# A fused linear-attention and mixture-of-experts kernel: W2's splits behind the first batch's gates, and two first-layer steps ahead of the projection's second part

## The chip, the cores and the metric

The kernel runs on one core of a Trainium2 chip. The metric is the device time of one execution in microseconds. Three runs of the kernel before took 406.46, 407.17 and 407.32 us, a median of 407.17 us. The execution that was profiled took 406.74 us.

## The reference

Eight batches of 576 tokens and 8 heads pass through an attention with 32 memory slots, and each token then goes to the one best of 8 experts.

```python
a = softmax(phi, axis=2)                       # over the 576 tokens
k_m, v_m = einsum(a, k), einsum(a, v)          # 32 slots per head
attn = softmax(q @ k_m.T / 8)                  # over the 32 slots
x = (attn @ v_m), heads side by side           # [4608, 512]
logits = xn @ en.T / tau                       # x and the 8 expert vectors, normed
expert_idx = argmax(logits); gate_w = softmax(logits)[expert_idx]
out[mask] = gate_w[mask] * (relu(x[mask] @ w1[e]) @ w2[e])
```

Inputs and outputs are fp32: w1 is 8 x 512 x 1024, w2 is 8 x 1024 x 512.

## The kernel before, in words

**One batch, one expert.** The kernel treats each batch as if all its tokens went to one expert (`choose` takes the fullest one; `rest` repairs the others at the end). Since x is a product of attention weights and v_m, the first layer is computed as weights times (v_m times W1): `project` makes the product G of v_m and W1 in two parts of 512 columns each (PSUM tiles pg), and `first` multiplies it with the turned attention weights aT.

**Three matmuls for one fp32 product.** G, aT, the hidden layer and W2 are each split in a high part, rounded to a shorter format, and a low part, the difference: gh and gl, the two aT tiles, hh and hl, wh and wl. A product is high times high, high times low and low times high. `split_w` makes one of the eight row blocks of wh by a copy and of wl by a subtraction, both from w2s; `part` does the same for aT.

**Steps.** `first(b)` has 16 steps: two halves of 288 tokens by eight blocks of 128 hidden units. Step f of the first half needs the columns of G from 128 f on, so steps 0 to 3 need only the first part of the projection. Each ends in an ACT copy with Relu (hh), in the second half another (h4, the last 64 tokens), and a DVE subtraction (hl). `second(b)` has 40 steps: eight for the last 64 tokens, which use w2s and h4 unsplit, then eight for each of four tiles of 128 tokens, which use wh, wl, hh and hl. `must(f)` makes a block of W2's split if the list has not yet done so.

**What stands between the steps.** `steps` fills two lists, `first` and `second`, with calls that are made behind the step of that number. They hold the rest of this batch's routing (`attend`, `norm`, `late`: norms, root, gates) and the next batch's attention: scores (ts, tl), their softmax over the slots in x on DVE and ACT (`fill` L64, `weigh` L71, L73, L75, `divide` L83 to L86), the turn into aw (`turn` L92, L94), and a copy of x by way of DRAM into ea (`lay`: eight td writes L100, then ea reads L104 and L106, which wait for all eight writes). Two batches ahead it takes the softmax of phi in ex (`largest` L457, `softmax` L472). `visit` turns ex on PE (L504) and multiplies aw with the values (`pairs` L139); `gather` chooses the next batch's expert (`choose`: ki L208, seli L209) and then calls for its weights: SP reads seli and issues four loads of W1 (w1s, L442) and four of W2 (w2s, L448).

**What sets the order.** The order in which the program calls is the order on each engine: PE, DVE, ACT, POOL (GpSimd) and SP, which issues nearly all DMAs, each take their own instructions strictly in that order and wait for semaphores. So on SP the ea reads, the two stores of `keep` (ad L633, vd L634) and the read of seli stand ahead of the next batch's W1.

**Before the change, batch 0.** Both parts of the projection and the attention of tiles 1 and 2 come ahead of the first step. Blocks 0 and 1 of W2 are split on POOL behind step 2, ahead of the gates' idx (L263); blocks 2 to 7 stand behind steps 9 to 14 on POOL, with the copies of 6 and 7 on ACT. The softmax of phi for batch 2 stands behind steps 18 and 21 of `second`.

Of the kernel before, what the change touches and what calls it, by code (L numbers as in the profile page):

```python
# [8 lines left out]
F32 = mybir.dt.float32  # L9
# [4 lines left out]
ALU = mybir.AluOpType  # L14
# [5 lines left out]
P = 128  # L20
B, H, S, D, M = 8, 8, 576, 64, 32
N, DM, E, FF = B * S, H * D, 8, 1024
NG = 2
# [5 lines left out]
HS = S // 2  # L29
# [246 lines left out]
class Kernel:  # L276
# [368 lines left out]
        for g in range(NG):  # L645
            self.part(g, slice(0, S))

    def split_w(self, copy=None):
        j = self.halves
        x, h, l = self.w2s[:, j], self.wh[:, j], self.wl[:, j]  # L650
        (copy or self.nc.scalar.copy)(h, x)  # L651
        self.nc.gpsimd.tensor_tensor(out=l, in0=x, in1=h.bitcast(F32), op=ALU.subtract)  # L652
        self.halves += 1

    def project(self, n, vT, room=None):
# [87 lines left out]
    def steps(self, b, t, u):  # L743


        first, second = ([[] for _ in range(n)] for n in (16, 40))

        for j in range(8):
            at = first[j] if b else first[2] if j < 2 else first[7 + j]
            at.append(lambda j=j: self.split_w(self.nc.gpsimd.tensor_copy if b or j < 6 else None))  # L750
        if not b:
            late = t.late()
            first[2].append(lambda: t.attend(3, 4))
            first[3].append(lambda: t.norm(3, 4))
            first[4] += [t.total, lambda: self.load_kv(2)]

            for f in range(3, 9):
                first[f].append(lambda: next(late))
            first[12] += [lambda: self.keep(0), lambda: self.load_q(2)]
        if u:  # L760
            c, o = b + 1, 0 if b else 3
            if not b:
                first[9].append(lambda: self.scores(c))
            for k in range(2):
                first[(3 + k if b else 9 + 2 * k)].append(lambda k=k: self.results(c, k))

            places = (first[6], first[8], first[10], first[12]), (first[12], first[14], second[0], second[3])
            if not b:
                places = (second[3], second[3], second[3], second[7]), (second[7], second[7], second[7], second[10])
            all = slice(0, BL)  # L770
            for g in range(NG):
                work = u.weigh((g,), all)
                places[g][0].append(lambda g=g: u.fill((g,), all, [self.sT[:, i] for i in range(NG)]))
                for at in places[g][1:]:
                    at.append(lambda work=work: next(work, None))
            for at, g in zip((second[0], second[3]) if b else (second[7], second[10]), range(NG)):
                at.append(lambda g=g: (u.divide((g,), all), u.lay(g), u.turn((g,), all)))
            o = 0 if b else 7
            m = b + 2
            if m < B:  # L780
                for g in range(NG):
                    second[11 + 3 * g + o].append(lambda g=g: self.softmax(m, (g,)))
                second[16 + o].append(lambda: self.shares(m))
                second[17 + o].append(lambda: self.visit(u, m))
                second[(20 if b else 19) + o].append(lambda: self.gather(u, m))
                second[(28 if b else 25) + o].append(lambda: self.load_phi(m + 1))
                second[(31 if b else 28) + o].append(lambda: self.load_kv(m + 1))
            else:
                second[17].append(u.attend)
                second[20].append(lambda: self.load_w2(u.choose()))  # L790
                second[37].append(lambda: list(self.project(c, self.vT[c % 2], self.pt)))
            o = 0 if b else 2
            second[22 + o] += [self.parts, lambda: self.keep(c)]
            second[23 + o + (not b)] += [u.owner, u.flags]
            for n, i in enumerate(((0, 1), (2, 3), (4,))):
                second[24 + n + o + (not b)].append(lambda i=i: u.norm(*i))
            after = u.late()
            for n in (27, 28, 29, 30, 31, 32):
                second[n + o].append(lambda: next(after))
            second[32 + o].append(lambda: list(after))  # L800
        return first, second
# [19 lines left out]
    def batch(self, b, t, u):  # L821

        first, second = self.steps(b, t, u)
        self.halves = 0

        def must(f):
            while self.halves <= f:
                self.split_w()

        if b and u:  # L830
            self.keys(b + 1)
            self.values(b + 1)
        for k, _ in enumerate(self.project(b, self.vT[b % 2]) if u else ()):
            if not b:
                for g in range(NG):
                    self.part(g, slice(HS, S) if k else slice(P, HS), self.nc.scalar.copy)
                if k:
                    t.norm(1, 2)
                else:
                    self.keys(1)  # L840
                    self.values(1)
                    t.attend(1, 2)
        if b and u:

            self.scores(b + 1)
        for n, _ in enumerate(self.first(b)):
            for step in first[n]:
                step()
        for n, _ in enumerate(self.second(b, self.gate[:, b], self.rows(b), must)):
            for step in second[n]:  # L850
                step()
            if n == 8 and b == B - 1:
                left = self.others()
            if n == 24 and b == B - 1:
                self.tc.mark_branch_hint_location("others", left[1], engines=[ET.PE, ET.DVE, ET.SP, ET.Activation])
        return left if b == B - 1 else None
# [244 lines left out]
```

## Time and profile before

| what | value |
|---|---|
| median of three runs | 407.17 us (406.46 to 407.32) |
| the profiled execution | 406.74 us, its span 404.9 us |
| granted clock of TensorE, mean | 0.998 of 2.4 GHz |
| PE busy | 393.5 us, 97% of the span |
| DVE busy | 262.3 us, 65% |
| ACT busy | 157.2 us, 39% |
| POOL busy | 171.2 us, 42% |
| moved by DMA | 91.24 MB, 225 GB/s on average |

The times in all rows are microseconds from the span's start. A batch takes about 45 us of it, and batch 0's first layer begins at 32.4 us. A matmul's end in the profile is modelled, so the start of the next one tells more than the end of the one before.

### The profile page before, as it was taken

To read this page: it belongs to the slowest core of one execution; us is meant where nothing else is said; L and a number is where in the kernel's file an instruction comes from. 1 tells how busy PE (TensorE), PEld (TensorE's weight loads), DVE (VectorE), ACT (ScalarE), POOL (GpSimd) and SP (SyncE) were. 2 spreads that over 40 slices of the span, in tenths; PEclk is the share of its full clock that TensorE was granted. 3 is DMA by queue.
4 is the path that set the end of the run, shared out by engine and by line. 5 is a ranking of instruction groups with operands and counts; after the bars stand their busy time and mean duration, and the time that the engine had idled before them with its cause. 6 is when DMAs were issued, how large, how long until landed. Compare 5 with 4: busy or idle time off the path is not lost. (4 is left out here: it accounts for less than half of the span.)

```text
span 404.9 us, 10350 instructions
## 1 busy us (share of the span) xinstructions
PE 393.5 (97%) x3933; PEld 318.5 (79%) x3933; DVE 262.3 (65%) x909; ACT 157.2 (39%) x430; POOL 171.2 (42%) x205
## 2 busy tenths in 40 slices
PE   7889999999999999999999999999999999999995
PEld 3458877798777978879787888879788897879784
DVE  4698795769664794758855795747936595745000
ACT  4366623165313633147311753137231561146110
POOL 1036563187133940369121961349303681329300
PEclk9999999999999999999999999999999999999999
DMA  8999927995679925995469926798359404790011
GB/s 265 345 363 357 375 61 183 342 358 212 149 255 386 349 46 132 346 384 234 74 215 389 387 82 160 251 388 338 56 137 361 178 2 81 249 396 6 14 53 56
DMA packets 69862, 91.24 MB, mean 225 GB/s; under 512 B 41800, under 2 KB 47688, under 8 KB 69808
## 3 DMA queue, kind: packets, MB, share of 16 engines
q1 hardware_dynamic: 66928, 82.00, 60.9%
q0 software_dynamic: 2688, 8.26, 5.8%
q8 instruction: 32, 0.52, 0.5%
q10 hardware_dynamic: 192, 0.28, 0.2%
q14 instruction: 22, 0.18, 0.1%
HBM read 71.19 MB, written 19.33 MB: 224 GB/s over the span
## 5 line engine op out<-in xcount | busy, mean ns | idle before, releaser
L681 PE MATMUL ph<-aT,gh 128*128 128x288 f32 x512 | 103.2, 297 | 0.0
L734 PE MATMUL py<-wh,hh 128*128 128x512 f32 x248 | 99.3, 400 | 0.0
L734 PE MATMUL py<-wh,hl 128*128 128x512 f32 x248 | 96.7, 390 | 0.0
L734 PE MATMUL py<-wl,hh 128*128 128x512 f32 x248 | 96.7, 390 | 0.0
L652 POOL TENSOR_TENSOR wl<-w2s,wh 128x512 fp32r<-128x512 f32 x64 | 85.1, 1330 | 5.0
L681 PEld LDWEIGHTS ph<-aT,gh 128*128 128x128 f32 x512 | 81.8, 188 | 1.7 <-DVE oh L162 0.8
L681 PE MATMUL ph<-aT,gl 128*128 128x288 f32 x256 | 75.4, 294 | 0.0
L687 DVE SCALAR_TENSOR_TENSOR hl<-ph,hh 128x288 fp32r<-128x288 f32 x128 | 55.8, 450 | 22.1 <-ACT hh L684 16.7
L739 ACT ACTIVATE ys<-py,gate 128x512 f32<-128x512 f32 (+1 forms) x39 | 25.1, 642 | 105.3 <-PE py L734 70.3
L684 ACT ACTIVATE hh<-ph 128x288 fp32r<-128x288 f32 x128 | 52.4, 417 | 31.9 <-PE ph L681 31.6
L868 POOL DMA_DIRECT2D out_dram<-ys x28 | 15.5, 553 | 106.1 <-ACT ys L739 69.4
L734 PEld LDWEIGHTS py<-wh,hh 128*128 128x128 f32 x248 | 46.5, 188 | 14.6 <-issue 4.9
L734 PEld LDWEIGHTS py<-wh,hl 128*128 128x128 f32 x248 | 46.6, 188 | 10.1
L734 PEld LDWEIGHTS py<-wl,hh 128*128 128x128 f32 x248 | 46.6, 188 | 9.0
L681 PEld LDWEIGHTS ph<-aT,gl 128*128 128x128 f32 x256 | 48.0, 188 | 0.0
L642 POOL TENSOR_TENSOR aT<-aw,aT 128x576 fp32r<-128x576 f32 (+3 forms) x20 | 23.7, 1204 | 48.4 <-DVE aT L641 42.8
L651 POOL CAST wh<-w2s 128x512 fp32r<-128x512 f32 x62 | 38.6, 622 | 1.0 <-DMA w2s<-w 0.9
L723 PE MATMUL py<-w2s,h 128*64 128x256 f32 x256 | 29.4, 382 | 0.0
L665 DVE TENSOR_TENSOR gl<-pg,gh 128x512 fp32r<-128x512 f32 x32 | 20.0, 684 | 8.7 <-ACT gh L664 8.7
L723 PEld LDWEIGHTS py<-w2s,h 128*64 128x64 f32 x256 | 17.7, 137 | 9.3 <-DVE hl L687 1.0
L472 ACT ACTIVATE ex<-ex,nm 128x576 f32<-128x576 f32 x16 | 12.3, 771 | 29.5 <-DVE nm L457 29.5
L664 ACT CAST gh<-pg 128x512 fp32r<-128x512 f32 x32 | 16.5, 599 | 10.5 <-PE pg L662 10.5
(180 smaller groups left out, 468.9 us busy)
## 6 DMA issues: line engine op xcount, KB each, us to landing
kx<-kv SPq DMA_DIRECT2D x32, 512.0 KB, 7.5
w2s<-w SPq DMA_DIRECT2D x32, 512.0 KB, 9.8
w1s<-w SPq DMA_DIRECT2D x28, 512.0 KB, 6.4
out_dram<-ys POOLq DMA_DIRECT2D x28, 256.0 KB, 6.1
qt<-qT SPq DMA_DIRECT2D x12, 576.0 KB, 8.8
ad<-aw SPq DMA_DIRECT2D x8, 576.0 KB, 12.5
td<-x SPq DMA_DIRECT2D x56, 72.0 KB, 2.1
ea<-td SPq DMA_DIRECT2D x7, 512.0 KB, 4.4
```

The costliest lines, as they stand in the source:

```text
L642: self.nc.gpsimd.tensor_tensor(out=al, in0=a, in1=ah.bitcast(F32), op=ALU.subtract)
L651: (copy or self.nc.scalar.copy)(h, x)
L652: self.nc.gpsimd.tensor_tensor(out=l, in0=x, in1=h.bitcast(F32), op=ALU.subtract)
L664: nc.scalar.copy(self.gh[:, g, f], ps[g])
L665: nc.vector.tensor_tensor(out=self.gl[:, g, f], in0=ps[g], in1=self.gh[:, g, f].bitcast(F32), op=ALU.subtract)
L681: nc.tensor.matmul(p, lhsT=w[:, g, fs], rhs=x[:, g, to], start=g == 0 and k == 0, stop=g == 1 and k == 2)
L684: nc.scalar.activation(self.hh[:, f, to], p, AF.Relu)
L687: nc.vector.scalar_tensor_tensor(out=self.hl[:, f, to], in0=p, scalar=0.0, in1=self.hh[:, f, to].bitcast(F32), op0=ALU.max, op1=ALU.subtract)
L723: nc.tensor.matmul(p[64 * j : 64 * j + 64], lhsT=self.h4[:, f], rhs=self.w2s[:, f, d * j : d * j + d], start=f == 0, stop=f == 7,)
L734: nc.tensor.matmul(p, lhsT=h[:, f, to], rhs=w[:, f], start=f == 0 and k == 0, stop=f == 7 and k == 2)
L739: nc.scalar.activation(y[:, :d], p, AF.Copy, scale=gate[:, i : i + 1])
L868: eng.dma_start(self.out[r : r + P], y)
```

## The change

In batch 0, W2's eight splits move behind steps 11 to 15 of `first` and steps 0 to 2 of `second`. Blocks 0 to 2 are copied by POOL and 3 to 7 by ACT; blocks 0 to 5 are subtracted by POOL and 6 and 7 by DVE. The projection's second part comes behind step 1 of `first`; the norms of tiles 1 and 2 come behind step 0. The late routing steps move by one step. The largest values of phi for batch 2 move from steps 18 and 21 of `second` to steps 0 and 1, and the exponentials to steps 2 and 5. For later batches the order on the engines stays as it was.

```diff
-    def split_w(self, copy=None):
+    def split_w(self, copy=None, by=None):
...
-        self.nc.gpsimd.tensor_tensor(out=l, in0=x, in1=h.bitcast(F32), op=ALU.subtract)
+        (by or self.nc.gpsimd).tensor_tensor(out=l, in0=x, in1=h.bitcast(F32), op=ALU.subtract)
...
-            at = first[j] if b else first[2] if j < 2 else first[7 + j]
-            at.append(lambda j=j: self.split_w(self.nc.gpsimd.tensor_copy if b or j < 6 else None))
+            at = first[j] if b else (first[11:] + second)[min(j, 7)]
+            copy = self.nc.gpsimd.tensor_copy if b or j < 3 else None
+            at.append(lambda j=j, copy=copy: self.split_w(copy, None if b or j < 6 else self.nc.vector))
...
-            first[2].append(lambda: t.attend(3, 4))
-            first[3].append(lambda: t.norm(3, 4))
-            first[4] += [t.total, lambda: self.load_kv(2)]
-
-            for f in range(3, 9):
+            first[3].append(lambda: t.attend(3, 4))
+            first[4] += [lambda: t.norm(3, 4), lambda: self.load_kv(2)]
+            first[5].append(t.total)
+
+            for f in range(4, 10):
                 first[f].append(lambda: next(late))
...
-                    second[11 + 3 * g + o].append(lambda g=g: self.softmax(m, (g,)))
+                    if not b:
+                        second[g].append(lambda g=g: self.largest(m, g))
+                    second[10 + 3 * g if b else 2 + 3 * g].append(lambda g=g: self.softmax(m, (g,)))
...
-        for k, _ in enumerate(self.project(b, self.vT[b % 2]) if u else ()):
-            if not b:
-                for g in range(NG):
-                    self.part(g, slice(HS, S) if k else slice(P, HS), self.nc.scalar.copy)
-                if k:
-                    t.norm(1, 2)
-                else:
-                    self.keys(1)
-                    self.values(1)
-                    t.attend(1, 2)
-        if b and u:
-
-            self.scores(b + 1)
+        project = self.project(b, self.vT[b % 2]) if u else ()
+        if b:
+            list(project)
+            if u:
+                self.scores(b + 1)
+        else:
+            self.part(0, slice(P, HS), self.nc.scalar.copy)
+            next(project)
+            self.part(1, slice(P, HS), self.nc.scalar.copy)
+            self.keys(1)
+            self.values(1)
+            t.attend(1, 2, turned=False)
+            first[0] += [lambda: t.turned(1, 2), lambda: t.norm(1, 2)]
+            first[1].insert(0, lambda: list(project))
+            for g in range(NG):
+                first[1].append(lambda g=g: self.part(g, slice(HS, S), self.nc.scalar.copy))
```

On DVE, at the end of batch 0's first layer: hl of the last step (ph_17), then the next batch's softmax over the slots (sT to x, the largest mx, the difference). The order before is this.

```order
L687 SCALAR_TENSOR_TENSOR hl<-ph_17_816,hh 128x288
L64 STREAM_TRANSPOSE x<-sT 128x576
L71 TENSOR_REDUCE mx_00_837<-x 128x18
L73 TENSOR_TENSOR x<-x,mx_00_837 128x576
L64 STREAM_TRANSPOSE x<-sT 128x576
```

The same place in the changed kernel, where nm is the largest of phi and wl the low part of W2:

```order
L687 SCALAR_TENSOR_TENSOR hl<-ph_17_808,hh 128x288
L457 TENSOR_REDUCE nm_826<-ex 128x1
L652 TENSOR_TENSOR wl<-w2s,wh 128x512
L457 TENSOR_REDUCE nm_826<-ex 128x1
L652 TENSOR_TENSOR wl<-w2s,wh 128x512
L64 STREAM_TRANSPOSE x<-sT 128x576
L71 TENSOR_REDUCE mx_00_843<-x 128x18
L73 TENSOR_TENSOR x<-x,mx_00_843 128x576
```

Two subtractions and the two largest values, which stood behind the whole softmax, now stand ahead of it.

On POOL, in batch 0's first layer, the difference of the two orders: the last two low parts of aT, then the gates' idx and W2's blocks.

```order
 L642 TENSOR_TENSOR aT_86<-aw,aT_85 128x160 x2
 L642 TENSOR_TENSOR aT_86<-aw,aT_85 128x288 x2
-L651 CAST wh<-w2s 128x512
-L652 TENSOR_TENSOR wl<-w2s,wh 128x512
-L651 CAST wh<-w2s 128x512
-L652 TENSOR_TENSOR wl<-w2s,wh 128x512
 L263 TENSOR_SCALAR idx<-m_209 128x5
 L651 CAST wh<-w2s 128x512
```

Two blocks no longer stand ahead of idx. Behind it stand three copies and six subtractions now, where four copies and six subtractions stood.

On PE, between the attention of tiles 1 and 2 (po) and the first layer (ph), before:

```order
L119 MATMUL po_1_520<-vv,aw 128x136 x2
L119 MATMUL po_2_523<-vv,aw 128x136 x2
L172 MATMUL tt_1_526<-ident,aw 128x128 x4
L662 MATMUL pg_10_536<-w1s,vT_80 32x512 x4
L662 MATMUL pg_11_537<-w1s,vT_80 32x512 x4
L681 MATMUL ph_00_556<-aT_85,gh 128x288
```

And in the changed kernel:

```order
L119 MATMUL po_2_523<-vv,aw 128x136 x2
L681 MATMUL ph_00_530<-aT_85,gh 128x288
L681 MATMUL ph_00_530<-aT_86,gh 128x288
L681 MATMUL ph_00_530<-aT_85,gl 128x288
L681 MATMUL ph_00_530<-aT_85,gh 128x288
L681 MATMUL ph_00_530<-aT_86,gh 128x288
L681 MATMUL ph_00_530<-aT_85,gl 128x288
L172 MATMUL tt_1_539<-ident,aw 128x128 x4
```

The first step of the first layer has moved ahead of the turned tile tt, and the projection's second part (pg_10, pg_11) behind the second step. SP's order is unchanged.

## Rows read from the trace of the kernel before

**Rows 1.** Page: busy time, share and instructions of PE.

```profile
PE 393.5 (97%) x3933; PEld 318.5 (79%) x3933; DVE 262.3 (65%) x909; ACT 157.2 (39%) x430; POOL 171.2 (42%) x205
```

**Rows 2.** Waits of PE from 27 us on: us in total, times, longest.

```profile
PE po L504 <- ACT ex L472: 0.6, 2, 0.5
PE tt L172 <- ACT kT L551: 0.4, 1, 0.4
PE pg L662 <- DMA w1s<-w: 0.3, 1, 0.3
PE acc L522 <- issue: 0.2, 1, 0.2
```

**Rows 3.** PE's timeline: start, us, instruction [idle before <-releaser].

```profile
64.40 0.28 PE L504 MATMUL po<-ident,ex 64*128 64x64 f32 x2 [0.46 <-ACT ex L472]
```

**Rows 4.** PE's weight loads for batch 1's projection.

```profile
80.42 0.23 PEld L662 LDWEIGHTS pg<-w1s,vT 64*32 64x32 f32 x10 [0.20 <-DMA w1s<-w]
```

**Rows 5.** DMA issues between 71.9 and 72.3 us: KB each, us to landing.

```profile
w1s<-w SPq DMA_DIRECT2D x1, 512.0 KB, 8.4
```

**Rows 6.** SP's timeline ahead of batch 1's W1.

```profile
58.13 5.12 SPq L100 DMA_DIRECT2D td<-x  x8
65.10 0.39 SPq L104 DMA_DIRECT2D ea<-td  x1
...
68.20 0.62 SPq L634 DMA_DIRECT2D vd<-vT  x1
70.30 2.70 SPq L442 DMA_DIRECT2D w1s<-w  x4
```

**Rows 7.** DVE's timeline, the number of batch 1's chosen expert.

```profile
68.56 0.14 DVE L209 TENSOR_SCALAR seli<-ki 1x1 int32<-1x1 int32 x1
```

**Rows 8.** DVE and SP, the same number and loads for batch 2.

```profile
111.97 0.14 DVE L209 TENSOR_SCALAR seli<-ki 1x1 int32<-1x1 int32 x1
```

**Rows 9.** SP, the loads of W1 for batch 2.

```profile
112.89 1.98 SPq L442 DMA_DIRECT2D w1s<-w  x4
```

**Rows 10.** DVE's timeline from batch 0's last step through batch 1's softmax.

```profile
49.59 0.46 DVE L687 SCALAR_TENSOR_TENSOR hl<-ph,hh 128x288 fp32r<-128x288 f32 x1 [0.47 <-ACT h L686]
49.97 0.77 DVE L64 STREAM_TRANSPOSE x<-sT 128x576 f32<-128x576 f32 x1
50.77 0.75 DVE L71 TENSOR_REDUCE mx<-x 128x18 f32<-128x576 f32 x1
51.56 1.56 DVE L73 TENSOR_TENSOR x<-x,mx 128x576 f32<-128x576 f32 x1
...
54.63 1.51 DVE L73 TENSOR_TENSOR x<-x,mx 128x576 f32<-128x576 f32 x1
56.06 0.74 DVE L83 TENSOR_REDUCE z<-x 128x18 f32<-128x576 f32 x1
...
60.28 0.76 DVE L86 TENSOR_TENSOR x<-x,z 128x576 f32<-128x576 f32 x1
...
61.98 0.71 DVE L457 TENSOR_REDUCE nm<-ex 128x1 f32<-128x576 f32 x1
```

**Rows 11.** POOL's timeline, W2's blocks in batch 0.

```profile
49.31 1.28 POOL L652 TENSOR_TENSOR wl<-w2s,wh 128x512 fp32r<-128x512 f32 x1
...
51.23 1.27 POOL L652 TENSOR_TENSOR wl<-w2s,wh 128x512 fp32r<-128x512 f32 x1
...
52.47 1.81 POOL L652 TENSOR_TENSOR wl<-w2s,wh 128x512 fp32r<-128x512 f32 x1
...
54.24 1.28 POOL L652 TENSOR_TENSOR wl<-w2s,wh 128x512 fp32r<-128x512 f32 x1
```

**Rows 12.** ACT's timeline, the last two steps of batch 0's first layer.

```profile
48.40 0.72 ACT L651 CAST wh<-w2s 128x512 fp32r<-128x512 f32 x1
48.91 0.53 ACT L684 ACTIVATE hh<-ph 128x288 fp32r<-128x288 f32 x1
```

**Rows 13.** PE's timeline, tile 0 of batch 0's second layer, block 5.

```profile
55.85 0.39 PE L734 MATMUL py<-wl,hh 128*128 128x512 f32 x1
```

## The prediction

> **What bounds the kernel now.** I read the page's busy times first: PE is busy for 393.5 of 404.9 us [rows 1], so time is won or lost only where PE stands still. Then PE's waits from the start of batch 0's projection on [rows 2]. After 27 us there are four groups of them, 1.5 us in all. The change reaches two: 0.4 us ahead of tt, and 0.46 us at 64.40 us, where PE wants to turn ex and ACT's exponential is late [rows 3]. If nothing else happened, the change could give back some 0.8 us, 0.2% of the run.
>
> So I looked for waits that almost exist. One stands in PE's weight loads: at 80.42 us batch 1's projection waited 0.20 us for the DMA of W1 [rows 4]. The fourth of W1's four loads was issued at about 72.0 us and landed 8.4 us later, at 80.4 [rows 5]: PE reached it just as it landed. There is no slack, and whatever delays that load delays everything behind it, since PE has no longer waits later on which the loss could be won back.
>
> What releases the load? SP takes its queue in order [rows 6]: the eight td writes of the next batch's softmax x, the last four of them behind the second half's L86; ea at 65.10, which waits until all td writes have landed; ad and vd, the latter's issue ending at 68.82; the reading of seli; W1 at 70.30. The number seli was ready at 68.70 [rows 7]. In batch 2, where SP stands waiting for it, W1 follows 0.78 us after seli is ready (112.89 less 112.11) [rows 8, 9]. By that way W1 could have gone at 69.5 in batch 1; it went at 70.30. So it is SP's own queue, and through td the DVE's softmax, that sets W1's issue. This chain runs from DVE at 60.28+0.76 = 61.04 us [rows 10] over td, ea, ad, vd and seli to W1's landing at 80.4 and PE.
>
> **The change part by part.**
>
> *The first steps ahead of the projection's second part.* The work of PE is the same, in another order; step 0 fills the 0.4 us in which tt waited for a PSUM copy [rows 2]. It needs gh, gl and aT of the first part, which may come 0 to 0.4 us late; gain between 0 and 0.4 us. I take 0.4: PE is then early by that through batch 0.
>
> *POOL.* Two blocks of W2 go from ahead of idx to behind it. DVE loses two stumbles against them, and gains a step's delay of the gates, so I leave idx where it was. The next three pairs then end as before, at 49.31+1.28 = 50.59 us [rows 11], and three bare subtractions of 1.28 us follow: 51.9, 53.2 and 54.4 undisturbed.
>
> *ACT.* One copy of W2 (0.51 us to the next start [rows 12]) goes from ahead of the last hh, and PE is 0.4 us early, so the last hl may start some 0.6 us sooner than 49.59 and end at 49.4 instead of 49.97. Then come four copies in a row at 0.51 us. The last hh (48.91 before [rows 12], some 0.6 us sooner) and its h4 take 0.4 us of ACT, so the first copy starts at about 48.75; that makes block 6's high part ready at 50.5 and block 7's at 51.0. The two exponentials of ex follow and are off the chain.
>
> *DVE.* Two largest values (0.69 us each, by 0.71 of L457 [rows 10]) and two subtractions, for which no row of DVE exists. The nearest is L86, two SBUF inputs and 576 columns: 0.76 us [rows 10]; for 512 columns 0.6 to 0.7 us, I take 0.6. The bound on the other side is what such an operation takes beside POOL: L73, of L86's shape, took 1.56 and 1.51 us [rows 10]. The first started at 51.56 while POOL subtracted from 51.23 to 52.50 and ended 0.62 us after that; the second started at 54.63, POOL ended at 55.52, and it ended 0.62 us later at 56.14. POOL's subtraction in between took 1.81 instead of 1.28 us [rows 11]. So each waits until the other's instruction is over. L64 and L71 kept their 0.77 and 0.75 us beside POOL.
>
> The Trainium skill ("SBUF — State Buffer", section "SBUF: two separate sides") says the same as a rule: VectorE and GpSimd share one pair of ports as an exclusive lock, which a VectorE instruction with two SBUF inputs needs and which is held for a whole instruction. This trace agrees, by the 0.62 us after POOL's end twice. It speaks against giving DVE two of the subtractions while POOL still makes the others: by the rule the sum is the second one below, and without it the first.
>
> First sum, nothing waits for POOL: hl ends 49.4, largest 50.1, subtraction from 50.5 (block 6's high part) to 51.1, largest 51.8, subtraction 52.4, then 0.80, 0.79 and 0.70 us twice for L64, L71 (start to start [rows 10]) and L73 (L86's 0.76 less a short overlap with the next): 57.0, where L83 starts. Before it started at 56.06 [rows 10]: +0.9 us. Second sum: the first subtraction waits for POOL's 50.59 and ends 51.2; largest 51.9; POOL's fourth runs from 51.15 to 52.43; the second subtraction ends 53.0; POOL's fifth ends 54.25 and its sixth starts at once; L64 and L71 are done at 54.6, L73 waits until 55.5 and ends 56.15; 0.80, 0.79, 0.70 more make 58.4: +2.4 us. That is .09, .55 and .91 us of lock beside the 0.9. If the phase is the worst, one more of POOL's 1.28 us falls in, less what L73 is spared: up to +3.4. I take +2.4, since the L73 rows show the lock at work in this very stretch.
>
> *Softmax of phi early.* ex is ready long before 64.40, so the 0.46 us goes [rows 3]. What is late next there is aw: the turns were done by 61.98 [rows 10], now 64.4, while PE, early by 0.8, wants them at about 64.2: 0.2 us comes back.
>
> *SP and PE.* From L86 on, every instruction of DVE and SP is the same and in the same order, so td, ea, ad, vd, seli and W1 all shift by the same 2.4 us: W1 is issued at 72.7 instead of 70.30, and its fourth load lands at 82.8 instead of 80.4. seli, earlier by some 0.6 us, decides nothing. PE comes to the projection 0.6 us sooner and stands there the longer. The early gains are swallowed: what counts is only the landing, +2.4 us. W2, phi and kv are issued behind W1 and shift with it, as PE does.
>
> *The last W2 block on POOL.* It ends at about 55.5 now; PE reads it at 55.85 before [rows 13], 55.5 with the 0.4 us gained. A wait here of 0.1 us, or of 1 us if POOL yields more often, is swallowed by W1's as well.
>
> The profiled execution's 406.74 us become 409.1; it was 0.43 us under the median of the three runs, so on the median's footing 407.17+2.4 = 409.6 us. (A difference of 0.2%, 0.8 us, is about what a measurement of this kernel tells from none.)
>
> **The rivals.**
>
> *W1 does not hold PE.* For it: the load's 8.4 us is long, and with other traffic around it could land sooner; a 2.4 us later issue with a 6 us flight would cost nothing. Against it: everything that shares the queues with it (ad and vd ahead, W2 behind) shifts with it. Then only the early gains are left: 407.17-0.4-0.46+0.2 = 406.5 us, at best 406.3. Not slower. 15 in 100, most of it within 0.2%.
>
> *No lock, or a lucky phase.* DVE's subtractions fall between POOL's instructions: the first sum, +0.9 us, 408.1. Against it: POOL's instructions follow each other with hardly a gap until 55.5 [rows 11]. 15 in 100 for +0.8 to +1.6.
>
> *Bad phase.* Each of the three DVE operations just misses POOL: +3.4 us, 410.6. 10 in 100 for above +3.0.
>
> *The forecast*, +1.6 to +3.0 us, 408.8 to 410.2: 60 in 100.
>
> **How the numbers follow.** Likeliest is 409.6. The range from 407.7 to 410.5 leaves out most of the case without W1's wait and the end of the bad phase. Slower by over 0.2% (above 407.98): 0.60+0.10+most of 0.15, 0.82. Within 0.2%: 0.12. Faster by over 0.2%: only if the early gains all come and no wait follows, 0.06.
>
> **What would show it.** Right: L457, L652, L457, L652 on DVE ahead of L64, the second L652 and one L73 over 1 us long beside POOL; L86's second half ending near 63.4; W1 issued near 72.7; a PE wait of 2 to 3 us at batch 1's projection, put down to the DMA of W1; no wait at tt and none for ex. Wrong: W1 issued near 70, or landing in time though issued late. A granted clock below 1.00 behind the new stop would push the time beyond the range.

## The result, and the profile after

| kernel | runs | median us | lowest to highest |
|---|---|---|---|
| before | 7 | 407.17 | 405.75 to 408.29 |
| after | 7 | 409.96 | 409.22 to 410.67 |

The ratio is 1.0071, with a 95% interval of 1.0053 to 1.009: the change costs 2.8 us. The forecast was 409.6 us, between 407.7 and 410.5.

The profiled execution of after took 410.67 us (span 408.9), the longest of its seven, and before's 406.74 was under its median. So the two traces differ by 3.9 us where the medians differ by 2.8. The granted clock is 1.00 in both. The page's first row answers to [rows 1]:

```profile
PE 397.0 (97%) x3933; PEld 319.0 (78%) x3933; DVE 262.4 (64%) x911; ACT 158.5 (39%) x433; POOL 167.4 (41%) x200
```

PE has the same 3933 matmuls and yet 3.5 us more of busy time. A matmul whose weights come late is partly counted as busy, so here the page hides a stall as work: the rows of PE for batch 1's projection are, in after and then in before,

```profile
79.94 1.98 PE L662 MATMUL pg<-w1s,vT 64*32 64x512 f32 x8
```

```profile
80.05 2.28 PE L662 MATMUL pg<-w1s,vT 64*32 64x512 f32 x32
```

and eight matmuls count for nearly as much as 32. The waits of PE from 27 us on (us in total, times, longest) show a part of it; they answer to [rows 2]:

```profile
PE pg L662 <- DMA w1s<-w: 1.6, 3, 0.8
PE acc L522 <- issue: 0.3, 1, 0.3
PE po L119 <- DVE aw L92: 0.2, 1, 0.2
```

The waits for ex and at tt are gone, as forecast. The other two need their places:

```profile
27.89 1.09 PE L662 MATMUL pg<-w1s,vT 64*32 64x512 f32 x16 [0.53 <-DMA w1s<-w]
30.27 0.96 PE L119 MATMUL po<-vv,aw 128*128 128x136 f32 x6 [0.15 <-DVE aw L92]
```

The wait for aw is one of batch 0's own attention. The forecast had one of 0.2 us for the next batch's aw at about 64 us, and there PE doesn't wait. Of the 1.6 us for W1, 0.5 are batch 0's first load, as the 0.3 us in before are (at 27.80 us); the other 1.1 us are new and stand at batch 1's projection. The full size of that stall is in the weight loads of batch 1's projection, which answer to [rows 4] (start, us, instruction, then in brackets the idle time before it and its releaser):

```profile
79.94 0.14 PEld L662 LDWEIGHTS pg<-w1s,vT 64*32 64x32 f32 x4 [0.17 <-PE tk L547]
80.88 0.14 PEld L662 LDWEIGHTS pg<-w1s,vT 64*32 64x32 f32 x4 [0.79 <-DMA w1s<-w]
82.75 0.14 PEld L662 LDWEIGHTS pg<-w1s,vT 64*32 64x32 f32 x4 [1.73 <-DMA w1s<-w]
84.04 0.19 PEld L662 LDWEIGHTS pg<-w1s,vT 64*32 64x32 f32 x16 [1.15 <-DMA w1s<-w]
```

The second, third and fourth of W1's four loads are now met while they are still under way, for 0.79+1.73+1.15 = 3.67 us, where before lost 0.20. Two rows of PE around this place, of after, fix what it cost:

```profile
79.41 0.38 PE L547 MATMUL tk<-ident,ks 128*128 128x128 f32 x2
...
86.98 0.53 PE L681 MATMUL ph<-aT,gh 128*128 128x288 f32 x2
```

The same two in before:

```profile
79.52 0.38 PE L547 MATMUL tk<-ident,ks 128*128 128x128 f32 x2
...
83.35 0.53 PE L681 MATMUL ph<-aT,gh 128*128 128x288 f32 x2
```

PE came to the projection 0.11 us earlier than before and left it 3.63 us later. At the end of the span the difference is 4.0 us: 3.74 of it arise in these few microseconds.

Where the chain that releases W1 lost its time is read on DVE, from batch 0's last step through batch 1's softmax, which answers to [rows 10]:

```profile
49.70 0.46 DVE L687 SCALAR_TENSOR_TENSOR hl<-ph,hh 128x288 fp32r<-128x288 f32 x1 [0.47 <-ACT h L686]
50.08 0.74 DVE L457 TENSOR_REDUCE nm<-ex 128x1 f32<-128x576 f32 x1
51.25 0.77 DVE L652 TENSOR_TENSOR wl<-w2s,wh 128x512 fp32r<-128x512 f32 x1 [0.43 <-ACT wh L651]
51.94 0.74 DVE L457 TENSOR_REDUCE nm<-ex 128x1 f32<-128x576 f32 x1
52.61 1.10 DVE L652 TENSOR_TENSOR wl<-w2s,wh 128x512 fp32r<-128x512 f32 x1
...
55.22 1.51 DVE L73 TENSOR_TENSOR x<-x,mx 128x576 f32<-128x576 f32 x1
...
58.24 0.76 DVE L73 TENSOR_TENSOR x<-x,mx 128x576 f32<-128x576 f32 x1
...
63.14 0.76 DVE L86 TENSOR_TENSOR x<-x,z 128x576 f32<-128x576 f32 x1
```

The softmax's last half ends at 63.90 instead of 61.04, 2.9 us later. The last hl starts 0.11 us later than before, so the rest, 2.75 us, arose between these rows: 14.20 us from hl's start to L86's end instead of 11.45. And on SP, whose rows answer to [rows 6]:

```profile
60.99 6.07 SPq L100 DMA_DIRECT2D td<-x  x8
69.45 0.39 SPq L104 DMA_DIRECT2D ea<-td  x1
...
74.68 2.24 SPq L442 DMA_DIRECT2D w1s<-w  x4
```

From L86's end to ea it takes 5.55 us where it took 4.06; from ea to W1 5.23 where it took 5.20. W1 is issued 4.4 us later, and lands 3.6 us later (84.0 instead of 80.4), since its fourth load takes 7.6 us from issue to landing instead of 8.4.

### The profile page after: what moved, and what is told of

It reads as the page before. It is cut to its first block, busy times and chain, and to the rows that moved or that the text cites. A ratio compares the mean times of both kernels' runs of the same rounds, so it can differ in the third digit from the quotient of the medians.

```text
span 408.9 us, 10352 instructions
## 1 busy us (share of the span) xinstructions
PE 397.0 (97%) x3933; PEld 319.0 (78%) x3933; DVE 262.4 (64%) x911; ACT 158.5 (39%) x433; POOL 167.4 (41%) x200
## 5 line engine op out<-in xcount | busy, mean ns | idle before, releaser
L652 POOL TENSOR_TENSOR wl<-w2s,wh 128x512 fp32r<-128x512 f32 x62 | 81.6, 1317 | 4.8
```

The source lines that it names most:

```text
L652: (by or self.nc.gpsimd).tensor_tensor(out=l, in0=x, in1=h.bitcast(F32), op=ALU.subtract)
```

## The experiments

All were timed beside before, whose medians in the three sessions were 406.8, 406.78 and 407.18 us. Each ratio is to before, with its 95% interval; after's is 1.0071. Three places of the chain, worked out from the profile of each (the starts of rows and their durations, as above), are used below:

| kernel | last hl starts | from there to L86's end | from there to ea | W1 issued |
|---|---|---|---|---|
| before | 49.59 | 11.45 | 4.06 | 70.30 |
| before, three idle reductions | 49.21 | 11.98 | 4.07 | 70.44 |
| before, W1 by ACT | 49.41 | 11.43 | 4.16 | 70.13 |
| before, six idle reductions | 49.88 | 13.85 | 4.24 | 73.39 |
| subtractions on POOL | 48.75 | 13.10 | 4.24 | 69.92 |
| phi's softmax late | 49.10 | 14.21 | 4.32 | 73.79 |
| before's places, keep late | 51.22 | 11.66 | 4.52 | 70.34 |
| without blocks 3 to 5 | 48.23 | 13.02 | 5.17 | 70.19 |
| without tile 1's store | 49.26 | 14.22 | 5.22 | 73.43 |
| fetches moved | 48.53 | 14.20 | 5.33 | 72.46 |
| W1 early | 48.97 | 14.20 | 5.54 | |
| after | 49.70 | 14.20 | 5.55 | 74.68 |
| W1 by ACT | 48.72 | 14.23 | 5.73 | 68.69 |
| keep late | 48.33 | 14.20 | 5.78 | 71.06 |

**W1 taken out of the chain.** From after; batch 1's W1 is loaded at the start of batch 0's second layer, from expert 0, so batch 1 is computed with that expert's first layer instead of the chosen one's.

```diff
-        k.load_w1(e, b == 0)
+        if b != 1:
+            k.load_w1(e, b == 0)
...
+            second[2].append(lambda: self.load_w1(0))
```

> The changed kernel, with batch 1's W1 fetched behind step 2 of second, from expert 0 whatever batch 1's choice is, so that it no longer hangs on seli, td, ea, ad and vd (batch 1 is computed with that expert's first layer). Theory (the whole loss is the late W1): no stop at batch 1's projection, all the early gains stay, 405.8 to 406.8 us where the kernel before has 406.8 to 407.2. Rival (the moved splits or the order of the projection cost by themselves): 408 us or more.

405.15 us, 0.9957 [0.9941, 0.9972]. L86's second half still ended at 63.17 and ea went at 68.71, 2.1 and 3.6 us later than in before; all that is left of PE's waits after 27 us is the first batch's own:

```profile
PE pg L663 <- DMA w1s<-w: 0.3, 1, 0.3
```

So a late softmax costs nothing by itself: the whole loss passes through W1. The gain of 1.6 us is more than expected. In this trace PE comes to the tk row at 78.68 us and to the ph row behind the projection at 82.18. That is 0.84 us ahead of before at the first row, 0.33 more between the two, where before still lost a little to W1, and the last 0.4 us come behind them. So what the change gains ahead of W1 is only a part of the 1.6 us.

**W1 ahead of ad and vd.** From after; the storing of ad and vd (`keep`) goes behind the gather in batch 0, so that W1 follows ea directly on SP.

```diff
-            second[22 + o] += [self.parts, lambda: self.keep(c)]
+            second[22 + o].append(self.parts)
+            second[22 + o if b else 27].append(lambda: self.keep(c))
```

> The changed kernel, with batch 1's two stores ad and vd (keep) behind the loads of W1 and W2 on SP instead of ahead of them. Theory (SP's queue holds W1): the reading of seli follows the ea reads directly, W1 is issued some 1.5 to 2 us earlier than in the changed kernel (at about 73 instead of 74.68 us), its landing and PE's stop move by as much, and the time falls from 409.96 to 408.0 to 408.5 us. Rival (the DMA engines' throughput or something behind SP holds the load): within 0.3 us of the changed kernel's 409.96.

407.65 us, 1.0024 [1.0, 1.0048]. SP's queue:

```profile
68.31 0.39 SPq L104 DMA_DIRECT2D ea<-td  x1
68.75 1.43 SPq L106 DMA_DIRECT2D ea<-td  x2
71.06 2.29 SPq L442 DMA_DIRECT2D w1s<-w  x4
```

And PE's weight loads, at the last quarter of W1:

```profile
80.57 0.18 PEld L662 LDWEIGHTS pg<-w1s,vT 64*32 64x32 f32 x16 [1.69 <-DMA w1s<-w]
```

The way from ea to W1 is 2.75 us instead of 5.23, W1 lands by 80.57 instead of 84.04, and 1.9 of after's 2.8 us come back: 0.85 us are left by the medians, 0.24% by the ratio. DVE's part of the delay is untouched here, so W1's place in SP's queue is as much a part of the chain as the softmax.

**The two subtractions given back to POOL.** From after:

```diff
-            at.append(lambda j=j, copy=copy: self.split_w(copy, None if b or j < 6 else self.nc.vector))
+            at.append(lambda j=j, copy=copy: self.split_w(copy))
```

> The changed kernel, with the low parts of W2's blocks 6 and 7 made by POOL again instead of DVE. Theory (DVE's softmax sets W1's issue): DVE loses 0.77+1.10 us of subtraction and 0.43 us of wait, but POOL works some 2.5 us longer and may hold both L73; L86's second half ends 1 to 2 us earlier, W1 goes as much earlier, and the time is 408.0 to 409.0 us; PE waits 1 to 2 us in tile 0 for the last blocks of wl, and that costs nothing, because it is taken off the stop at W1. Rival (the late blocks of wl are the price): the wait in tile 0 comes on top, 410 us or more.

407.54 us, 1.0016 [0.9995, 1.0037]. DVE needs 13.10 us from hl to L86's end: 1.1 less than after, 1.65 more than before: the largest values are still there (L64 starts 1.69 us behind hl's start instead of 0.38), both L73 are long again (1.60 and 1.51 us), and a small operation, L84, takes 0.47 instead of 0.18 us beside POOL. W1 is in time, and PE's waits are other ones:

```profile
PE py L734 <- POOL wl L652: 0.8, 1, 0.8
PE pg L662 <- DMA w1s<-w: 0.3, 1, 0.3
PE po L504 <- ACT ex L472: 0.2, 1, 0.2
```

POOL then makes six subtractions in a row (8.56 us from 49.23) and the last block comes 0.8 us late for tile 0. The rival, that this wait comes on top, is out. That price, which the change avoids by using DVE, is smaller than the one that it pays.

**POOL's subtractions beside DVE left out.** From after; in batch 0 POOL doesn't subtract for W2's blocks 3 to 5, whose low parts hold other numbers written once at the start.

```diff
-        (by or self.nc.gpsimd).tensor_tensor(out=l, in0=x, in1=h.bitcast(F32), op=ALU.subtract)
+        if not (first and 2 < j < 6):
+            (by or self.nc.gpsimd).tensor_tensor(out=l, in0=x, in1=h.bitcast(F32), op=ALU.subtract)
...
```

> The changed kernel without POOL's low parts of W2's blocks 3, 4 and 5 in batch 0 (their wl is filled with other numbers at the start). Theory (the shared port is held for a whole instruction): with POOL idle from about 50.5 us on, DVE's second subtraction takes 0.6 to 0.8 instead of 1.10 us and the first L73 0.76 instead of 1.51 us, L86's second half ends 1.0 to 1.3 us earlier against the last hl, and the time is 408.2 to 409.2 us, less if td then clears the tile 1 store. Rival (no lock, these durations belong to the instructions): durations and time as in the changed kernel, 409.96 within 0.3 us.

407.68 us, 1.0022 [1.0003, 1.0042]. DVE's two L73:

```profile
53.32 0.76 DVE L73 TENSOR_TENSOR x<-x,mx 128x576 f32<-128x576 f32 x1
...
55.59 0.76 DVE L73 TENSOR_TENSOR x<-x,mx 128x576 f32<-128x576 f32 x1
```

With POOL silent no operation is long, and the way is 13.02 us: 1.57 over before's 11.45, and 1.18 under after's. This takes the 2.75 us apart. DVE's own added work (two largest values, two subtractions, and 0.42 us of waiting for ACT's high part) puts L64 3.50 us behind hl's start instead of 0.38, which is 3.12 more; that both L73 are short gives back 1.55. In after the lock takes 0.43 us of the second subtraction and 0.75 of one L73, 1.18 together. So before had more of the lock (1.55 us) than after: what the change adds is DVE's own work, and the lock only keeps that work from being paid for by the L73 that come free. The Trainium skill ("SBUF — State Buffer", section "SBUF: two separate sides") has the rule, an exclusive lock between a VectorE instruction with two SBUF inputs and a GpSimd one; these rows agree, 0.76 us without POOL and 1.51 with it. The kernel's median falls with it, to 407.68 from 409.96 us, and by more than the 1.18: in this trace the way from L86's end to ea is also 0.38 us shorter than in after, and that from ea to W1 1.46 (70.19 less 66.42, for 5.23). The lock's own share of the median is not separated from these.

**The softmax of phi back in its old place.** From after:

```diff
-                    if not b:
-                        second[g].append(lambda g=g: self.largest(m, g))
-                    second[10 + 3 * g if b else 2 + 3 * g].append(lambda g=g: self.softmax(m, (g,)))
+                    second[10 + 3 * g if b else 18 + 3 * g].append(lambda g=g: self.softmax(m, (g,)))
```

> The changed kernel, with the largest values and the exponentials of phi for batch 2 back behind steps 18 and 21 of second, as before the change. Theory (every DVE instruction ahead of the softmax counts): DVE has 0.74+0.74 us less ahead of it, but the first subtraction waits for ACT's block 6 all the same, so L86 ends 0.7 to 1.5 us earlier and the time is 408.4 to 409.2 us, with PE's wait for ex of some 0.4 us back and swallowed. Rival (only the two subtractions and the lock count): within 0.3 us of 409.96.

409.96 us, 1.007 [1.0048, 1.0091]: nothing gained, against the theory and as the rival said. DVE's way is 14.21 us, as in after: without the largest values between them, the two subtractions took the same time, 1.08 us of idle for ACT's high part and 2.47 us for both. And the largest values now stand behind the late softmax, so that PE waits for the exponential:

```profile
66.67 0.28 PE L504 MATMUL po<-ident,ex 64*128 64x64 f32 x2 [2.85 <-ACT ex L472]
```

W1, issued at 73.79, then costs PE only the 0.20 us that it cost before. Its last quarter lands at 84.23 us, so without the wait for ex PE would have stood for W1 instead.

The early softmax of phi costs DVE nothing, it fills waits; and it guards PE from a late ex as long as DVE is late.

**Idle work on DVE, in before.** Three reductions of 576 columns ahead of batch 1's softmax, and in a second kernel six:

```diff
...
+                for k in range(3):
+                    second[k].append(self.idle)
```

> The kernel before, with three needless DVE reductions of 576 columns (some 0.72 us each, 2.2 us) in batch 0 behind steps 0, 1 and 2 of second, ahead of the softmax, where the change put its four. Nothing else is changed. Theory (DVE to td to SP to W1 to PE, without slack): +1.6 to +2.2 us less what L73 is spared beside POOL, 408.6 to 409.4 us, and a stop of PE for W1 at batch 1's projection. Rival (DVE has slack there; the loss comes from the moved splits or the projection's order): within 0.3 us of 407.17.

> The kernel before with six needless DVE reductions (0.69 us each from start to start, 4.1 us) ahead of the softmax in batch 0. With three of them L86 shifted by only 0.15 us, because both L73 then missed POOL's subtractions and lost 1.5 us of wait. With six nothing is left to be spared: L86 shifts by 2.3 to 2.8 us against the last hl, W1 by as much or up to 1.5 us more. Theory (DVE to td to SP to W1 to PE): 409.2 to 411 us, ratio 1.005 to 1.010. Rival (a later softmax alone does not hold PE): within 0.4 us of the kernel before.

Three: 407.31 us, 1.0006 [0.9988, 1.0023], where a loss was expected. DVE's rows:

```profile
49.58 2.06 DVE L406 TENSOR_REDUCE idle<-sT 128x1 f32<-128x576 f32 x3
...
53.15 0.85 DVE L73 TENSOR_TENSOR x<-x,mx 128x576 f32<-128x576 f32 x1
...
55.52 0.76 DVE L73 TENSOR_TENSOR x<-x,mx 128x576 f32<-128x576 f32 x1
```

The 2.06 us pushed both L73 past POOL's instructions. They took 0.85 and 0.76 us instead of 1.56 and 1.51 [rows 10], so that 1.46 us came back and the way grew by only 0.53; hl was 0.38 us early, and L86 ended 0.15 us later than before. (In this trace PE loses 1.19 us to W1 even so, since the fourth load took 9.3 us to land; the median shows no loss.) Six: 410.46 us, 1.0098 [1.0077, 1.0118]; with no lock left to win, the way is 2.40 us longer and W1 goes at 73.39. But this loss is not W1's alone, since PE first waits, ahead of the projection, for the exponential behind the late softmax:

```profile
PE po L508 <- ACT ex L476: 2.9, 1, 2.9
PE tt L172 <- ACT kT L555: 0.4, 1, 0.4
PE pg L666 <- DMA w1s<-w: 0.3, 1, 0.3
```

```profile
83.93 0.18 PEld L666 LDWEIGHTS pg<-w1s,vT 64*32 64x32 f32 x16 [1.03 <-DMA w1s<-w]
```

PE comes to the tk row at 82.21 us, 2.69 later than in before, and then still loses 1.03 us to W1, where before lost 0.20. So this run confirms that a later DVE there is paid for, first at the exponential and for the rest at W1.

**W1 issued by ACT.** The number of the expert is read, and W1 of batch 1 issued, on ACT instead of SP, in after and in before:

```diff
-        k.load_w1(e, b == 0)
+        if b == 1:
+            x = nc.scalar.value_load(k.seli[:, b : b + 1], min_val=0, max_val=E - 1)
+            k.load_w1(x, eng=nc.scalar)
+        else:
+            k.load_w1(e, b == 0)
...
```

> The changed kernel with batch 1's W1 read and issued by ACT, which stands idle from 66 to 70 us, instead of by SP behind td, ea, ad and vd; SP still loads W2. Theory (only SP's queue makes W1 late): W1 is issued about 69 us, 0.8 to 1.5 us after seli is ready, and lands before PE comes to batch 1's projection; no stop, all the early gains stay, 405.2 to 406.2 us, 0.2 to 0.4% under the kernel before. Rival (its data competes with ea, ad and vd and lands late all the same): 407 us or more.

> The kernel before with batch 1's W1 read and issued by ACT. Theory (before the change W1 lands just as PE comes to it): almost nothing to win, 0 to 0.5 us under the kernel before. Rival (PE already loses over a microsecond to W1 in usual runs of the kernel before): 0.8 us or more under it.

In before: 406.8 us, 1.0012 [0.9991, 1.0033], no difference, as expected. In after: 407.93 us, 1.0035 [1.0013, 1.0057], the rival's time. W1 goes at 68.69, 6 us earlier than in after, and another wait takes its place; PE's waits of that kernel:

```profile
PE pg L666 <- ACT ys L743: 1.7, 1, 1.7
PE pg L666 <- DMA w1s<-w: 0.3, 1, 0.3
```

ea's data, now on the way together with W1's, come late: its reads take 6.1 and 7.5 us to land instead of 4.2 and 4.0 in after, and DVE waits for them until 77.68 us, in after until 73.65. So the routing norms on DVE are late, ACT stands at the gates' exponential until 81.90, and the scaling ys behind it frees PSUM too late:

```profile
81.90 0.24 ACT L262 ACTIVATE l<-l 128x40 f32<-128x40 f32 x1 [7.94 <-DVE l L260]
82.05 0.67 ACT L743 ACTIVATE ys<-py,gate 128x512 f32<-128x512 f32 x1
```

In the weight loads PE still loses 0.84 us to W1 at 79.99 us, and then 2.60 to ys.

**The way from L86 to ea.** Two causes were tried for the extra 1.5 us, both from after: without the store of batch 0's tile 1 (those rows of the output stay unwritten), and with 30 short matmuls at the start, which move the fetches of instructions in time.

```diff
+            elif i < NT - 1 and (b, i) != (0, 1):
+                eng.dma_start(self.out[r : r + P], y)
             elif i < NT - 1:
-                eng.dma_start(self.out[r : r + P], y)
+                pass
```

```diff
     k.warm(11)
+    k.warm(30, hot=k.mm([P, 512], "hot", 0)[:, :4])
```

> The changed kernel without the store of batch 0's tile 1 (256 KB; those rows of the output are left unwritten). Theory (the later td writes now run into this store, which costs the 1.5 us by which the way from L86's end to the first ea read grew, 4.06 to 5.55 us): that way is 4.0 to 4.4 us again, W1 is issued 1.0 to 1.5 us earlier, 408.4 to 409.2 us where the changed kernel has 409.96. Rival (td is slow for another reason, W1 shifts by DVE's delay alone): within 0.3 us of 409.96, and the way still over 5 us.

> The changed kernel with 30 more matmuls of 4 columns at the very start, behind the first 11 that warm PE up; PE's instruction stream is 60 instructions longer ahead of everything else. In the changed kernel one packet of the instruction queue q8 (16 KB) falls into the second half of td's writes, which land 3.7 us after issue instead of 2.2. Theory (that packet holds one DMA engine and td waits for its slowest): the packet comes some 6 us earlier, clear of td's second half, the last td writes land in 2.2 to 2.6 us, ea starts 4.1 to 4.5 us after L86's end instead of 5.55, and the time falls by 1 to 1.4 us from 409.96, to 408.5 to 409.0. Rival (td's longer flight has another cause): the way from L86 to ea stays above 5 us and the time within 0.4 us of 409.96.

Without the store: 411.48 us, 1.0107 [1.0068, 1.0146], and the way is 5.22 us; with the fetches moved: 409.35 us, 1.0074 [1.0052, 1.0096], and it is 5.33 us. The ratios are no better than after's, and both ways stay above 5 us, as the rivals said: neither alone is the cause. In the table the way is 4.06 to 4.5 us in seven kernels and 5.2 to 5.8 in seven. In the traces of the longer ones tile 1's store, a packet of 16 KB of the instruction queue, or both run while the last td writes do; in the shorter ones neither does, or just at their end (before's places, keep late, and the subtractions on POOL). One kernel made from after is among the shorter, phi's softmax late: there the last td write lands at 67.50 us, the store is issued at 67.48 and the packet starts at 67.78, and the way is 4.32 us with DVE as late as in after. So either one being enough fits all fourteen. No kernel was made to take away just these two, so it is not shown. Without the store W1 went 1.25 us earlier than in after, but its fourth load took 9.1 us to land instead of 7.6, and PE met its last quarter at 84.25 us, in after at 84.04. Why the load took longer, and the kernel was slower still than after, stays open.

**The rest of the change with before's places for W2.** From after, with before's places for the splits, and ad and vd late as above:

```diff
-            at = first[j] if b else (first[11:] + second)[min(j, 7)]
-            copy = self.nc.gpsimd.tensor_copy if b or j < 3 else None
-            at.append(lambda j=j, copy=copy: self.split_w(copy, None if b or j < 6 else self.nc.vector))
+            at = first[j] if b else first[2] if j < 2 else first[7 + j]
+            at.append(lambda j=j: self.split_w(self.nc.gpsimd.tensor_copy if b or j < 6 else None))
```

> The changed kernel with all of W2's splits where and by which engines they were before, and with batch 1's stores ad and vd behind the loads of W1 and W2; the projection's order and the early softmax of phi stay. Theory: DVE has only the two largest values ahead of the softmax, SP gains 1.5 to 2 us, so W1 lands in time; no PE wait for W1 and none for ex, 405.8 to 406.6 us, 0.1 to 0.3% under the kernel before. Rival (the splits ahead of idx hold DVE in the gates and W1 is still late): 407 us or more.

407.22 us, 1.0008 [0.9987, 1.0028], the rival's time and half of its reason: W1 is not late. It is issued at 70.34 and no longer waited for, but waits in the first layer take the gain. A row of DVE there, and one of PE:

```profile
39.55 1.18 DVE L38 TENSOR_SCALAR nrg<-ss 128x5 int32<-128x5 int32 x1
```

```profile
41.69 0.53 PE L681 MATMUL ph<-aT,gh 128*128 128x288 f32 x2 [0.57 <-DVE hl L687]
```

POOL's subtractions stand among the gates again, and operations of 5 columns wait for them, 1.18 us for 0.17 in before; hl behind them is late, PE stops for 0.57 us, and the last hl starts at 51.22, 1.6 us after before's. No kernel that computes all of the reference was found to be faster than before.

## Why the prediction was right

*W1 without slack.* Right. The wait stands at batch 1's projection, for the DMA of W1, and taking W1 out of the chain turns a loss of 0.71% into a gain of 0.43%. The first rival, that W1 does not hold PE, falls with this run, though its point about the flight, the time from issue to landing, was partly true: the fourth load's was 0.8 us shorter.

*The lock.* Right, by the rows it named: the second subtraction took 1.10 us, one L73 1.51, the other 0.76. From hl's start to L83's the second sum had 9.5 us (58.4 less 48.94, 0.46 ahead of hl's end at 49.4) and after took 9.21. The first sum, without POOL, had 8.1 where before took 6.47, or 1.6 more; with POOL's subtractions left out the way is 1.57 us longer. The rival without a lock falls by that. In the forecast's account of the difference the last of the three pieces of lock, 0.91 us, is 0.1 too large for its own rows: 0.09+0.55+0.91 give 1.55, its two sums differ by 1.4.

*L86's end.* Predicted 2.4 us later, measured 2.9 in after's profile. The way was 0.25 us shorter than summed, but the last hl, which was to start 0.65 us early, started 0.11 late. Seven other kernels that keep the change's order up to that hl had it at 48.33 to 49.26, early by 0.3 to 1.3 us, around the 0.65 of the forecast. In after's own execution DVE waited 1.72 us near the start, where 0.27 in before's (L38, in code that is the same in both), and was still 1.07 us behind at batch 0's L86. Over the fourteen traces this wait is 0.26 to 1.72 us, after's being the longest. So it is most likely chance of one execution, and a reason why its trace is slower than the median; no second trace of after was taken.

*From L86 to W1.* Here a step failed: that td, ea, ad, vd, seli and W1 "all shift by the same". From L86's end to ea it did not hold, by 1.5 us, and what made td longer is not shown. From ea to W1 it held to 0.03 us in after, but by luck: in the kernels that leave SP's order as it was, this way is 3.8 to 6.2 us. Nor is the fourth load's flight a constant: 7.3 to 9.3 us in the kernels in which SP issues it. In after W1 was issued 4.4 us later, not 2.4, and landed 3.6 us later.

*The early gains.* They were put at 0.4 us for the first steps and 0.46 for ex, less 0.2. With W1 out of the way the kernel gains 1.6 us, of which 0.84 stand ahead of the projection. In the seven kernels that keep the change's order and in which PE waits neither for ex nor for a block of W2, after among them, it comes to the tk row 0.1 to 1.6 us earlier than in before's trace, 1.06 in the middle one. The 0.2 us that aw was to cost did not come. Which gain was larger is not separated; a candidate is what the prediction set off as even, the stumbles of DVE against POOL's two blocks ahead of idx, which took 0.92 and 0.63 us at two small operations of the gates in before and are 0.18 and 0.17 in after. They stay out of the total, as forecast, since PE only stands longer at W1.

So the median came out at 409.96 for 409.6 partly by luck, because errors cancel. The kernel with the fetches moved, which differs from after in a few short matmuls at the start, shows it without after's late start: DVE's way 2.75 us longer, hl 1.06 early, td to ea 1.27 longer, ea to W1 0.80 shorter, W1 issued at 72.46 and its last quarter met by PE at 82.81, where the prediction had 72.7 and 82.8. The longer way to ea is made up there by an earlier hl and a shorter way from ea to W1, of which the forecast had the first only in part and the second not at all.

## What to carry to other kernels

Look in the weight loads, too, for a transfer that lands just as PE reaches it: a wait of 0.2 us there can mean that the chain which issues that transfer has no slack left. Work moved onto an engine which looks free in the page has to be priced in the stage where it lands and along the chain that it stands in: DVE was busy 65% of the span, and yet two subtractions ahead of one softmax, with the wait for what they read, started a loss of 2.8 us; the two maxima beside them filled that wait and cost nothing. And a stall can sit in PE's busy time: compare when the same instruction starts in both traces, ahead of a suspected place and behind it.

## What the runs showed of the hardware that was not expected

In the kernel before, more DVE work hardly lengthened the chain: 2.06 us of reductions, which don't wait for POOL, moved two L73 out of POOL's way and gave 1.46 us back. Beside POOL's subtractions the operations with two SBUF inputs waited, but also tiny ones with one (TENSOR_SCALAR of 5 columns, 1.18 us for 0.17); reductions (0.74 us) and transposes (0.77 us) kept their times.

Eight td writes of 72 KB, the same in every kernel, took 4.1 to 5.8 us from the last softmax operation to the read behind them. What else the queues carried at that time differed; that this is the reason fits the traces and is not shown.
